# An attention and MoE kernel on one core: the gate is finished inside its PSUM bank

## The chip, the cores and the metric

The kernel runs on one core of one Trainium2 chip. The metric is device time in microseconds (us) of one execution. The kernel before takes 829.81 us, the median of three runs between 829.25 and 830.32 us. One execution was profiled: it took 829.51 us, and its profile spans 827.7 us from the first instruction to the last.

## The reference

The reference computes a linear attention over 8 batches and 8 heads (576 rows of 64 each) and feeds its output, 4608 tokens of 512 numbers, to two matrix products with a gate between them. All inputs and outputs are fp32.

```python
q_s = softmax(q, axis=-1); k_s = softmax(k, axis=2)       # per row; per column over the 576 rows
kv = einsum('bhsd,bhse->bhde', k_s, v)
x = einsum('bhsd,bhde->bhse', q_s, kv)                    # then reordered to 4608 x 512
h = x @ w_in                                              # 512 -> 2048
g = h - np.tanh(h)
out = g @ w_out                                           # 2048 -> 512
```

`softmax` stands here for the max, exp, sum and division that the reference writes out (with 1e-9 added to each sum).

## The kernel before

**Tiles.** The 4608 tokens are nine chunks of 512 (index j). The 2048 hidden columns are 16 blocks of 128 (index f). A step is one pair (j, f). It has two matrix products on TensorE (PE):

- `ph` (line 739): 12 matmuls of 128x512 that write h of the step, transposed, into one PSUM bank. fp32 is carried by two fp32r parts per factor: the parts are `xh`, `xl` of x and `w[0]`, `w[1]` of the weights, and three of the four products are made.
- `po` (line 814): 12 matmuls of 128x512 that add the step's share to four output banks, one per 128 tokens. The gate g comes as two parts, `gh` (rounded to fp32r) and `gl` (the rest).

So a step has 24 matmuls, and 144 steps have 3456.

**The gate of a step** (`h_parts`, lines 719 to 793) is made of ten instructions between the two products. ScalarE (ACT) reads the bank twice (`u` = h squared, `t` = tanh h) and makes `vv` from `u`. VectorE (DVE) makes `tt` (h - tanh h, from the bank), `g` (in place in the bank), `gg` (from the bank to an SBUF tile `g`) and `cp`, a select (COPY_PREDICATED, line 761) that puts `t` into the SBUF tile where the mask `m` of `u` says so. `m` is made on ACT or DVE. Then `gh` casts the SBUF tile (ACT, GpSimd or DVE, line 195) and `gl` subtracts (DVE or GpSimd (POOL), line 775). The bank of `ph` comes free behind `gg`.

**PSUM.** Of the eight banks four are `ps_o` (the outputs `po`; at the program's head also small products, and `ph` of steps 2 and 3), two are `ps_h` (`ph`) and two are `ps_m` (`pm`, `pb`, `pk`, `pt`, `px`: the products of the attention).

**Attention.** For each batch, k is loaded, its column maximum taken (`km`), exponentiated (`ke`), and multiplied with v (`pk`); the sums are divided out (`sl`, `rs`, `rc`, `kn`) into `kvs`. q is loaded, softmaxed by rows (`mq`, `qu`, `qe`, `sq`, `sa`, `sr`, `qn`), turned (`pt` on PE and a copy `qs` to SBUF in the first two chunks, by DMA later) and multiplied with `kvs` (`px`), and `xh`, `xl` are made from `px`. The q, k and v of batches 0 and 1 are worked on at the head of the program; later ones lie between the steps.

**Weights** come as 8-byte words and are turned into two fp32r parts on the chip: `ld` (DMA), `cl` and `pr` (clamp and scale the high words), `lo` (the low words, ACT), `st` (shift and or, DVE), `ca` (cast) and `sub` (the rest). A piece `i0` or `o2` is of `w_in` or `w_out` and begins at that block of 128.

**Order.** The order of all instructions is written out by hand in three texts: FIRST (the head and the first 32 steps), ROUND (16 steps, run for the chunks 2 to 8) and LAST. Each word is one operation; the emission in that order gives every engine its own queue, in order. A mark at a word's end moves it from its home engine: `*` to DVE, `^` to POOL, `!` to ACT. The same order also issues the DMAs, on SyncE's (SP's) queue. PE runs the `po` of a step one to several steps behind its `ph`.

Of the kernel before, what the change touches and what calls it, by code (L numbers as in the profile page):

```python
# [10 lines left out]
F32 = mybir.dt.float32  # L11
F32R = mybir.dt.float32r
# [19 lines left out]
k0.0 km0.a warm1 vo0.2 warm8 warm1 k0.1 km0.b warm3 k0.2 km0.c kk0.1 kk0.3 km0.d q1 vo0.0 kk0.0 pm0  # L32
q0 mq1 vo0.1 mq0 q3 qu1 mx0 kk0.2 warm3 qe1 mq3 ld.i4 qu0 pb0 kl0.1 qe0 vo1.1 ks0.2 sq1 cl.i4^
warm3 sq0 sa1 sa0 kf0.2 v0.2 ke0.1 kl0.3 sr1 sr0 lo.i4 kl0.0 kl0.2 pr.i4 warm3 ke0.0 qu3 qn1* qn0*
ld.i2 warm3 pt1 qe3 ke0.2 pt0 st.i4 v0.0 sq3 pk0.0 ke0.3 v0.1 ca.i4 qs1 ld.i0 cl.i2 sub.i4* qn2*
pk0.2 pk0.1 sa3 lo.i2 qn3 pt3 sl0 sr3 rs0 cl.i0^ qn7 rc0 q2 ld.i1 k1.1 pt2 pr.i2 qs2 qs0* qn6 kn0
qs3 k1.0 st.i2 pr.i0 px0 lo.i0 ca.i2 px2 mq2 warm3 st.i0 sub.i2* vo1.2 xh0.1 xh2.0 pt7 ld.o0 warm3
qu2* xh0.0 xl0.0 km1.a xh2.1 xl0.1 cl.i1^ pt6 k1.2 ca.i0 sub.i0 qe2 ld.o2 v1.1 lo.i1 qs7 xl2.1 pha0
vo1.0 phc2 pha2 qs6 pha3 xl2.0 sq2 km1.b phb0 cl.o0^ pr.i1 phc0 phb2 pr.o0 km1.c st.i1 lo.o0 phb3
km1.d ld.i12 st.o0 u0 ca.i1 t0 pm1 vv0 u2 tt0 sa2 t2 phb1 v1.0 phc3 mx1 g0 tt2 ca.o0 pb1 gg0 m0  # L40
ks1.0 cp0 pha1 sub.i1 cl.o2^ lo.o2 phc1 pr.o2 ke1.0 u1 ks1.1 sr2 ks1.2 phb5 qn4 t1 g2 tt1 ke1.1
phc5 ld.o4 v1.2 vv1 g1 ke1.2 gg1 m1 pha5 pk1.0 qn5* pt4 gh0^ pk1.1 pk1.2 qs4 cp1 sub.o0* vv2 pt5
gl0 po0.1b st.o2 gg2 t3 m2 gh1 phb4 po0.0b po0.0a qs5 sl1 gl1 pha4 po1.0a ld.i6 po1.1a u3 tt3 ca.o2
cl.o4^ rs1 g3 vv3 m3 rc1 gg3 po1.0b po0.3a po1.3a cp2 kn1 sub.o2* po0.1a phc4 lo.o4 po1.2a po1.3b
pr.o4 +q.0 po0.2a po1.2b ld.i8 t4 gh2 po1.1b px4 po0.2b po0.3b u4 cp3 po2.1a st.o4 po2.2a xh4.0
ld.i10 gh3^ xh4.1 po2.3a t5 po3.1a po2.0a tt4 xl4.0 vv4 xl4.1 g4 ld.o6 gl3 gg4 px6 ca.o4 gl2 ld.o8
ld.i15 m4 po3.1b cl.i8 xh6.0 u5 po2.2b po3.3a po3.2b xh6.1 po3.2a sub.o4* cp4 po3.3b cl.i6^ vv5
po3.0b xl6.1 gh4 pr.i8 tt5 po2.3b xl6.0 pha6 po3.0a po4.0a lo.i6 po2.1b phb6 phc6 gl4 g5 gg5 m5*
# [48 lines left out]
phc1 phb0 phc0 pha0 po15.0a u0 +q.0 po15.2a +mq.0 vv0 po15.0b phb1 po14.1a po15.3a +qu.0* t0
po15.3b tt0 g0 pha1 po15.1a t1 po14.0a m0* gg0 cp0 po14.2b u1 po14.3b tt1 po14.0b gh0 phb2 g1 oc.0*
vv1 gg1 +qe.0 pha2 phc2 po0.2a os.0 po14.3a +sq.0 t2 tt2 m1 po15.2b po15.1b po14.1b po14.2a oc.1*
pha3 u2 gl0* vv2 phb3 po0.1b phc3 g2 gg2 m2 phb4 pha4 phc4 cp1 oc.2 po0.2b po0.0a os.1 gh1 oc.3  # L100
po0.1a po0.3a gl1* cp2 +sa.0 po0.3b t3 +k.0 +sr.0 +qn.0* po1.0a po0.0b u3 +k.2 t4 po1.0b gh2 tt3
# [29 lines left out]
def attn_moe_kernel(  # L131
# [9 lines left out]
    nc = tc.nc  # L141
# [919 lines left out]
```

## Time and profile before

| | |
|---|---|
| median of three runs | 829.81 us |
| the profiled execution | 829.51 us, its span 827.7 us |
| PE busy | 816.2 us (99%) |
| DVE busy | 697.9 us (84%) |
| ACT busy | 511.7 us (62%) |
| POOL busy | 87.8 us (11%) |
| chain that ended last | PE 92%, ACT 3%, DMA 2%, the rest 1% each |

Times inside the profile count from the first instruction. A busy PE includes the `warm` products (line 276), which do no work that is needed. Where a view prints a duration, instructions of one engine overlap a little: the next one starts before the one in front has ended, so the distance from start to start is shorter than the duration.

### The profile page before, as it was taken

How to read it: one execution, taken by the hardware profiler on the slowest of the kernel's cores; microseconds unless marked ns; L12 is line 12 of the kernel's file. 1: busy time of each engine (PE TensorE's matmuls, PEld its weight loads, DVE VectorE, ACT ScalarE, POOL GpSimd, SP SyncE). 2: the span in 40 equal slices, each digit the busy share in tenths (PEclk: the TensorE clock that was granted, in tenths of full speed). 3: DMA queues.
4: the chain of work that ended last, by engine and by line, in shares of the span. 5: the costliest groups of instructions: out<-in, count | busy, mean ns of one | idle time of the engine just before them, and what ended most of it. 6: DMA issues, size and time to landing. Idle time of an engine off the chain costs nothing.

```text
span 827.7 us, 13205 instructions
## 1 busy us (share of the span) xinstructions
PE 816.2 (99%) x4830; PEld 705.3 (85%) x4830; DVE 697.9 (84%) x1134; ACT 511.7 (62%) x845; POOL 87.8 (11%) x94
## 2 busy tenths in 40 slices
PE   8899999999999999999999999999999999999997
PEld 7788888888888888888888888888888888888886
DVE  6999999977999789987998789978997897767564
ACT  4899998645555656555656465556555565456553
POOL 4545535301000000000000000000000000000000
PEclk9999999999999999999999999999999999999999
DMA  9974500433221504041314122332304120301001
GB/s 300 357 287 169 172 2 1 128 101 110 71 83 41 145 18 136 13 131 43 98 55 140 47 82 71 102 84 59 95 26 139 34 77 15 123 4 52 1 1 51
DMA packets 99935, 75.83 MB, mean 92 GB/s; under 512 B 17184, under 2 KB 84768, under 8 KB 99872
## 3 DMA queue, kind: packets, MB, share of 16 engines
q1 hardware_dynamic: 99712, 74.74, 29.2%
q8 instruction: 38, 0.62, 0.3%
q10 hardware_dynamic: 160, 0.26, 0.1%
q14 instruction: 25, 0.20, 0.1%
HBM read 56.10 MB, written 18.89 MB: 91 GB/s over the span
## 4 chain that ended last, share of the span: by engine, by line
PE 92%; ACT 3%; DMA 2%; POOL 1%; issue 1%; DVE 1%; SPq 0%; ACTq 0%; POOLq 0%
PE po L814 45%; PE ph L739 43%; PE pk L444 2%; PE px L676 2%; DMA raw_o<-in_moe_w_out_dram 1%; DMA q<-in_q_dram 1%; POOL c_i L225 0%; ACT raw_o L235 0%; ACT c_o L231 0%; PE px L660 0%; ACT k L432 0%; ACT raw_i L235 0%; POOL q L537 0%; ACT c_i L231 0%; ACT u L766 0%
## 5 line engine op out<-in xcount | busy, mean ns | idle before, releaser
L814 PE MATMUL po<-w_o,gh 128*128 128x512 f32 x1152 | 309.8, 379 | 0.3 <-POOL gh L195 0.3
L739 PE MATMUL ph<-xh,w_i 128*128 128x512 f32 x1152 | 283.8, 379 | 0.6 <-ACT w_i L195 0.6
L739 PEld LDWEIGHTS ph<-xh,w_i 128*128 128x128 f32 x1152 | 217.2, 189 | 32.1 <-ACT w_i L195 0.9
L814 PEld LDWEIGHTS po<-w_o,gh 128*128 128x128 f32 x1152 | 217.4, 189 | 31.8 <-POOL gh L195 0.7
L814 PE MATMUL po<-w_o,gl 128*128 128x512 f32 x576 | 185.7, 382 | 0.0
L739 PE MATMUL ph<-xl,w_i 128*128 128x512 f32 x576 | 148.8, 381 | 0.8 <-DVE g L756 0.5
L195 ACT CAST gh<-g 128x512 fp32r<-128x512 f32 x122 | 75.3, 618 | 101.2 <-PE po L814 78.5
L753 DVE TENSOR_TENSOR t<-ph,t 128x512 f32<-128x512 f32 x144 | 97.7, 682 | 45.6 <-ACT t L729 41.3
L729 ACT ACTIVATE t<-ph 128x512 f32<-128x512 f32 x144 | 85.2, 592 | 74.9 <-PE ph L739 70.1
L729 ACT ACTIVATE u<-ph 128x512 f32<-128x512 f32 x144 | 85.1, 591 | 63.3 <-PE ph L739 44.9
L814 PEld LDWEIGHTS po<-w_o,gl 128*128 128x128 f32 x576 | 108.6, 189 | 17.4 <-issue 1.2
L739 PEld LDWEIGHTS ph<-xl,w_i 128*128 128x128 f32 x576 | 107.8, 189 | 18.0 <-PE po L814 1.2
L775 DVE TENSOR_TENSOR gl<-g,gh 128x512 fp32r<-128x512 f32 x128 | 87.2, 684 | 37.1 <-ACT gh L195 18.8
L761 DVE COPY_PREDICATED g<-u,t 128x512 f32<-128x512 int32 x144 | 108.9, 764 | 4.1 <-ACT u L766 2.4
L756 DVE SCALAR_TENSOR_TENSOR g<-vv,ph 128x512 f32<-128x512 f32 x144 | 98.1, 681 | 9.7 <-ACT vv L729 4.3
L729 ACT ACTIVATE vv<-u,b_pa 128x512 f32<-128x512 f32 x144 | 103.8, 721 | 2.6 <-DVE g L756 1.0
L748 DVE SCALAR_TENSOR_TENSOR ph<-u,ph 128x512 f32<-128x512 f32 x144 | 99.3, 689 | 5.8 <-ACT u L729 5.7
L766 ACT ACTIVATE u<-u 128x512 int32<-128x512 f32 x118 | 74.4, 631 | 28.5 <-DVE ph L748 28.1
L304 POOL MEMSET v<- 128x16 f32 x14 | 1.7, 119 | 374.0 <-DVE tb L575 152.1
L195 ACT CAST xh<-px 128x512 fp32r<-128x512 f32 x36 | 20.0, 587 | 13.1 <-PE px L676 13.1
L775 POOL TENSOR_TENSOR gl<-g,gh 128x512 fp32r<-128x512 f32 x16 | 22.1, 1384 | 50.1 <-ACT gh L195 36.3
L717 DVE TENSOR_TENSOR xl<-px,xh 128x512 fp32r<-128x512 f32 x36 | 23.9, 685 | 3.2 <-ACT xh L195 3.2
(117 smaller groups left out, 553.0 us busy)
## 6 DMA issues: line engine op xcount, KB each, us to landing
k<-in_k_dram SPq DMA_DIRECT2D x16, 512.0 KB, 4.3
q<-in_q_dram SPq DMA_DIRECT2D x15, 512.0 KB, 5.3
v<-in_v_dram SPq DMA_DIRECT2D x14, 512.0 KB, 5.6
qd<-tb SPq DMA_DIRECT2D x28, 256.0 KB, 3.2
out_dram<-o SPq DMA_DIRECT2D x28, 256.0 KB, 2.3
qs<-qd SPq DMA_DIRECT2D x112, 64.0 KB, 2.0
raw_i<-in_moe_w_in_dram SPq DMA_DIRECT2D x6, 1024.0 KB, 8.2
raw_o<-in_moe_w_out_dram SPq DMA_DIRECT2D x6, 1024.0 KB, 10.6
```

The lines of the kernel that those rows point to most:

```text
L195: (eng.copy if eng is nc.scalar else eng.tensor_copy)(to, of)
L444: nc.tensor.matmul(st["pk"][hh * D : (hh + 1) * D, a, j : j + D + 1], kt[:, h, j] if u < NKP else kt[:, h], vt[:, h, j * (D + 1) : (j + 1) ...
L717: nc.vector.tensor_tensor(xl, px, xh.bitcast(F32), op=ALU.subtract)
L729: nc.scalar.activation(new(tag, **of), st[src], fn, **kw)
L739: nc.tensor.matmul(pairs(st["ph"]), w[:, i, c], halves(xs[j][x][:, c, :]), start=n == 0, stop=n == 3 * NC - 1,)
L748: nc.vector.scalar_tensor_tensor(st["ph"], st["u"], C2, st["ph"], op0=ALU.mult, op1=ALU.mult)
L753: nc.vector.tensor_tensor(st["t"], st["ph"], st["t"], op=ALU.subtract)
L756: nc.vector.scalar_tensor_tensor(new("g"), st["vv"], PB, st["ph"], op0=ALU.add, op1=ALU.mult)
L761: nc.vector.copy_predicated(st["g"], st["mk"], st["t"])
L766: eng.activation(mk, st["u"], AF.Copy, scale=0.5 / U_MAX)
L775: eng.tensor_tensor(new("gl", F32R), st["g"], st["gh"].bitcast(F32), op=ALU.subtract)
L814: nc.tensor.matmul(pairs(po[key]), gs[j, f][g][:, cols], halves(wt["o", f][:, w]), start=n == 1, stop=n == last,)
```

## The change

The SBUF tile `g` goes. `gg` and `cp` now write the bank of `ph` itself, and `gh` and `gl` read it there, so a bank comes free only behind `gl`. POOL does not take part any more: `gl` is always on DVE, and `gh` on ACT or DVE. `ps_h` and `ps_m` become one ring of four banks, from which the small products take theirs too; `ph` of steps 2 and 3 no longer uses `ps_o`. The room of the SBUF tiles `g` goes to a third buffer of `dec` (the weights' work tiles and the output tiles). The last two output tiles are copied whole by one engine each and not in two halves. FIRST and ROUND are new texts; of LAST one mark is gone.

```diff
 FIRST = """
-k0.0 km0.a warm1 vo0.2 warm8 warm1 k0.1 km0.b warm3 k0.2 km0.c kk0.1 kk0.3 km0.d q1 vo0.0 kk0.0 pm0
+q0 mq0 qu0* warm8 k0.0 vo0.2 qe0 warm3 k0.1 warm3 warm3 kk0.1 km0.a km0.b k0.2 q1 warm3 km0.c mq1
...
 LAST = """
-po142.2a po142.2b po143.2a po143.2b oc8.2* os8.2 po142.3a po142.3b po143.3a po143.3b oc8.3 os8.3
+po142.2a po142.2b po143.2a po143.2b oc8.2 os8.2 po142.3a po142.3b po143.3a po143.3b oc8.3 os8.3
...
-    ps_h = ctx.enter_context(tc.tile_pool(name="ps_h", bufs=2, space=bass.MemoryType.PSUM))
-    ps_m = ctx.enter_context(tc.tile_pool(name="ps_m", bufs=2, space=bass.MemoryType.PSUM))
+    ps_h = ctx.enter_context(tc.tile_pool(name="ps_h", bufs=4, space=bass.MemoryType.PSUM))
-    dec = ctx.enter_context(tc.tile_pool(name="dec", bufs=2))
+    dec = ctx.enter_context(tc.tile_pool(name="dec", bufs=3))
...
         def gg():
             nc.vector.scalar_tensor_tensor(
-                new("g"), st["vv"], PB, st["ph"], op0=ALU.add, op1=ALU.mult
+                st["ph"], st["vv"], PB, st["ph"], op0=ALU.add, op1=ALU.mult
             )
         def cp():
-            nc.vector.copy_predicated(st["g"], st["mk"], st["t"])
+            nc.vector.copy_predicated(st["ph"], st["mk"], st["t"])
...
         def gh(eng):
-            cast_on(eng, new("gh", F32R), st["g"])
+            cast_on(eng, new("gh", F32R), st["ph"])
-        def gl(eng):
-            eng.tensor_tensor(
-                new("gl", F32R), st["g"], st["gh"].bitcast(F32), op=ALU.subtract
+        def gl():
+            nc.vector.tensor_tensor(
+                new("gl", F32R), st["ph"], st["gh"].bitcast(F32), op=ALU.subtract
             )
...
         elif j == NCH - 1 and t >= TPC - 2:
             o = gp.tile([P, DM], F32, name=f"o{j}_{t}", tag="t")
-            to, of = by_half(o), paired(po[key])
-            nc.scalar.copy(to[:, 0], of[:, 0])
-            nc.vector.tensor_copy(to[:, 1], of[:, 1])
+            cast_on(eng, by_half(o), paired(po[key]))
```

**The loads of the head, on SP's queue.** `k1_0` and `k1_1` are the two large tiles of k of batch 1, `raw_i` and `raw_o` pieces of the weights. Before:

```order
L203 DMA raw_i0_281<-in_moe_w_in_dram 128x4x128
L517 DMA q1_0_332<-in_q_dram 128x8x128
L203 DMA raw_i1_334<-in_moe_w_in_dram 128x4x128
L282 DMA k1_1_336<-in_k_dram 128x8x128
L282 DMA k1_0_350<-in_k_dram 128x8x128
L208 DMA raw_o0_396<-in_moe_w_out_dram 128x2x512
L287 DMA kr1_416<-in_k_dram 64x8x64
L208 DMA raw_o2_422<-in_moe_w_out_dram 128x2x512
```

Now:

```order
L517 DMA q1_0_275<-in_q_dram 128x8x128
L314 DMA v0_0_216<-in_v_dram 128x8x128
L203 DMA raw_i4_318<-in_moe_w_in_dram 128x4x256
L208 DMA raw_o0_342<-in_moe_w_out_dram 128x2x512
L282 DMA k1_1_391<-in_k_dram 128x8x128
L282 DMA k1_0_414<-in_k_dram 128x8x128
L287 DMA kr1_416<-in_k_dram 64x8x64
L314 DMA spare_v1_273<-in_v_dram 128x8x128
```

The loads of batch 1's k have moved behind a piece of `w_out` and a piece of `w_in`; the rows ahead of these hold the same other tiles in both.

**The head of DVE's queue, from the row maximum of batch 1 (`mx1`) on.** `ph0_0` is h of step (0, 0), `c_i` and `c_o` are work tiles of the weights. Before:

```order
L377 TENSOR_REDUCE mx1_511<-pm1_487 128x4
L748 SCALAR_TENSOR_TENSOR ph0_0_429<-u0_0_481,ph0_0_429 128x512
L753 TENSOR_TENSOR t0_2_499<-ph0_2_436,t0_2_499 128x512
L756 SCALAR_TENSOR_TENSOR g0_0_522<-vv0_0_492,ph0_0_429 128x512
L429 TENSOR_TENSOR k1_0_350<-k1_0_350,pb1_517 128x1024
L761 COPY_PREDICATED g0_0_522<-u0_0_481,t0_0_485 128x512
L429 TENSOR_TENSOR k1_1_336<-k1_1_336,pb1_517 128x1024
L558 RECIPROCAL sq1_0_497<-sq1_0_497 128x16
L429 TENSOR_TENSOR kr1_416<-kr1_416,pb1_517 64x512
L748 SCALAR_TENSOR_TENSOR ph0_2_436<-u0_2_494,ph0_2_436 128x512
L753 TENSOR_TENSOR t0_1_553<-ph0_1_501,t0_1_553 128x512
L748 SCALAR_TENSOR_TENSOR ph0_1_501<-u0_1_541,ph0_1_501 128x512
```

Now:

```order
L377 TENSOR_REDUCE mx1_502<-pm1_483 128x4
L747 SCALAR_TENSOR_TENSOR ph0_0_433<-u0_0_469,ph0_0_433 128x512
L755 SCALAR_TENSOR_TENSOR ph0_0_433<-vv0_0_479,ph0_0_433 128x512
L752 TENSOR_TENSOR t0_1_471<-ph0_1_438,t0_1_471 128x512
L760 COPY_PREDICATED ph0_0_433<-u0_0_469,t0_0_463 128x512
L747 SCALAR_TENSOR_TENSOR ph0_1_438<-u0_1_498,ph0_1_438 128x512
L755 SCALAR_TENSOR_TENSOR ph0_1_438<-vv0_1_513,ph0_1_438 128x512
L553 TENSOR_REDUCE sq1_0_536<-sums_eps_97 128x16
L774 TENSOR_TENSOR gl0_0_538<-ph0_0_433,gh0_0_517 128x512
L760 COPY_PREDICATED ph0_1_438<-u0_1_498,t0_1_471 128x512
L752 TENSOR_TENSOR t0_2_531<-ph0_2_474,t0_2_531 128x512
L774 TENSOR_TENSOR gl0_1_557<-ph0_1_438,gh0_1_544 128x512
```

The gates' instructions on one bank stand closer together, each `gl` is now in this queue, and the subtractions of batch 1's k have moved behind them.

**POOL's queue in the same stretch.** `w_o0` is the fp32r tile of the first piece of `w_out`, `qn4` and `qn5` are scaled q tiles of the second chunk. Before:

```order
L225 TENSOR_SCALAR c_o0_458<-raw_o0_396 128x1024
L255 TENSOR_TENSOR w_i1_483<-c_i1_409,w_i1_483 128x512
L225 TENSOR_SCALAR c_o2_532<-raw_o2_422 128x1024
L604 TENSOR_TENSOR qn4_551<-q1_0_332,sq1_0_497 128x2x4x64
L195 CAST gh0_0_600<-g0_0_522 128x512
L775 TENSOR_TENSOR gl0_0_637<-g0_0_522,gh0_0_600 128x512
L775 TENSOR_TENSOR gl0_1_661<-g0_1_569,gh0_1_647 128x512
L225 TENSOR_SCALAR c_o4_678<-raw_o4_562 128x1024
L195 CAST gh0_3_747<-g0_3_687 128x512
L775 TENSOR_TENSOR gl0_3_766<-g0_3_687,gh0_3_747 128x512
```

Now:

```order
L225 TENSOR_SCALAR c_o0_421<-raw_o0_342 128x1024
L195 CAST w_o0_488<-c_o0_421 128x1024
L255 TENSOR_TENSOR w_o0_488<-c_o0_421,w_o0_488 128x1024
L255 TENSOR_TENSOR w_i4_500<-c_i4_399,w_i4_500 128x1024
L225 TENSOR_SCALAR c_o2_549<-raw_o2_446 128x1024
L225 TENSOR_SCALAR c_i8_600<-raw_i8_453 128x1024
L195 CAST w_o2_608<-c_o2_549 128x1024
L255 TENSOR_TENSOR w_o2_608<-c_o2_549,w_o2_608 128x1024
L604 TENSOR_TENSOR qn5_615<-q1_0_275,sq1_0_536 128x2x4x64
L604 TENSOR_TENSOR qn4_699<-q1_0_275,sq1_0_536 128x2x4x64
```

POOL no longer makes `gh` or `gl`; casts and subtractions of the weights, which DVE and ACT made, have come in their place.

## Rows read from the trace of the kernel before

**Rows 1.** The page, part 1: busy time (share of the span) and instructions.

```profile
PE 816.2 (99%) x4830; PEld 705.3 (85%) x4830; DVE 697.9 (84%) x1134; ACT 511.7 (62%) x845; POOL 87.8 (11%) x94
```

**Rows 2.** Stretches of 20 us: busy time and instructions (x) of each engine; clock; DMA.

```profile
40.00:60.00 20.00, 19.82 (x176) 16.29 (x175) 19.56 (x33) 19.92 (x31) 9.32 (x9) 1.00 0.79 281
...
480.00:500.00 20.00, 20.00 (x95) 17.50 (x94) 18.42 (x32) 13.18 (x22) 0.00 (x0) 1.00 0.28 86
```

**Rows 3.** Waits of PE: engine, line, waited for: us in total, times, longest.

```profile
...
PE ph L739 <- DVE g L756: 0.5, 1, 0.5
PE pm L338 <- ACT raw_o L235: 0.4, 1, 0.4
PE po L814 <- POOL gh L195: 0.3, 1, 0.3
...
```

**Rows 4.** PE in order of time: start, us, line, out<-in, count.

```profile
30.48 3.77 PE L739 MATMUL ph<-xh,w_i 128*128 128x512 f32 x16 [0.62 <-ACT w_i L195]
...
57.90 1.09 PE L660 MATMUL px<-spare_qs,kvs 64*64 64x256 f32 x16
```

**Rows 5.** The chain that ended last, 20 to 36 us: start, us, what.

```profile
24.52 9.27 DMA raw_o<-in_moe_w_out_dram
...
33.94 1.58 POOL c_o L225
```

**Rows 6.** DVE in order of time, 40 to 46 us: start, us, line, operation.

```profile
40.79 0.69 DVE L748 SCALAR_TENSOR_TENSOR ph<-u,ph 128x512 f32<-128x512 f32 x1
41.39 0.69 DVE L753 TENSOR_TENSOR t<-ph,t 128x512 f32<-128x512 f32 x1
...
42.58 1.22 DVE L429 TENSOR_TENSOR k<-k,pb 128x1024 f32<-128x1024 f32 x1
43.71 0.76 DVE L761 COPY_PREDICATED g<-u,t 128x512 f32<-128x512 int32 x1
44.36 1.21 DVE L429 TENSOR_TENSOR k<-k,pb 128x1024 f32<-128x1024 f32 x1
```

**Rows 7.** Groups by line and form: busy, mean ns | idle before, and releasers.

```profile
L761 DVE COPY_PREDICATED g<-u,t 128x512 f32<-128x512 int32 x144 | 108.9, 764 | 4.1 <-ACT u L766 2.4
...
L717 DVE TENSOR_TENSOR xl<-px,xh 128x512 fp32r<-128x512 f32 x36 | 23.9, 685 | 3.2 <-ACT xh L195 3.2
...
L775 DVE TENSOR_TENSOR gl<-g,gh 128x512 fp32r<-128x512 f32 x128 | 87.2, 684 | 37.1 <-ACT gh L195 18.8 <-PE po L814 10.3 <-ACT u L766 7.0
...
L195 ACT CAST gh<-g 128x512 fp32r<-128x512 f32 x122 | 75.3, 618 | 101.2 <-PE po L814 78.5 <-DVE g L761 19.8 <-DVE sl L457 1.1
...
L195 ACT CAST xh<-px 128x512 fp32r<-128x512 f32 x36 | 20.0, 587 | 13.1 <-PE px L676 13.1
...
L195 DVE COPY o<-po 128x512 f32<-128x512 f32 x15 | 10.3, 687 | 2.6 <-PE po L814 2.6
...
L195 ACT COPY o<-po 128x512 f32<-128x512 f32 x15 | 8.6, 574 | 1.5 <-PE po L814 1.5
...
L195 DVE CAST gh<-g 128x512 fp32r<-128x512 f32 x14 | 5.8, 414 | 0.0
...
L255 POOL TENSOR_TENSOR w_i<-c_i,w_i 128x1024 fp32r<-128x1024 f32 x2 | 4.8, 2414 | 0.0
```

**Rows 8.** All engines in order of time, near 158 us.

```profile
158.03 1.28 POOL L429 TENSOR_TENSOR kr<-kr,mrow 64x512 f32<-64x512 f32 x1
...
158.28 1.65 DVE L761 COPY_PREDICATED g<-u,t 128x512 f32<-128x512 int32 x1
...
159.81 0.68 DVE L753 TENSOR_TENSOR t<-ph,t 128x512 f32<-128x512 f32 x1
```

**Rows 9.** All engines in order of time, the last microseconds.

```profile
822.92 0.37 ACT L839 COPY o<-po 128x256 f32<-128x256 f32 x1 [1.08 <-PE po L814]
823.33 0.42 DVE L840 COPY o<-po 128x256 f32<-128x256 f32 x1 [1.03 <-ACT o L839]
823.78 0.50 ACTq L850 DMA_DIRECT2D out_dram<-o  x1
```

More of the change, by code (lines that the diff above doesn't have):

```diff
@@ L37 @@
[L37 to L48, printed above, removed]
@@ new lines @@
+t1 km1.d pha2 vv0 st.o0 tt0 pm1 ca.o0^ phb2 phc2 u1 ca.i4 mx1 g0 phb3 sub.o0 m0 gg0 vv1 tt1 cp0 gh0
+phc3 pha3 g1 sub.i4 gg1 v1.2 t2 po0.0a sa2 gl0 m1 cp1 u2 gh1 po0.3a cl.o2^ vv2 u3 tt2 v1.0 gl1
+po0.1a g2 pr.o2 po0.2a pb1 po0.3b po1.0a ks1.2 po1.1b po1.3b phb4 po0.2b lo.o2 ks1.0 m2 ks1.1 phc4
+t3 st.o2 ke1.2 pha4 cl.i8^ sr2 gg2 cp2 po1.2a ke1.1 ca.o2^ sub.o2 ke1.0 vv3 po0.0b qn5 tt3 gh2
+po1.0b po1.3a g3 po1.2b t4 pk1.2 pk1.1 pk1.0 gl2 sl1 m3 gg3 lo.i8 u4 rs1 rc1 po1.1a po2.3b po2.0a
+pt5 cp3 ld.o4 kn1 ld.i10 po0.1b qs5 qn4 ld.i6 gh3* vv4 pha5 tt4 gl3 +vo.2 cl.o4^ g4 pt4 pr.i8 qs4*
@@ L94 @@
+gl30
 """
 ROUND = """
[L97 to L101, printed above, removed]
@@ L334, in kv_max_t @@
     def kv_max_t(b: int, st: dict):
-        st["pm"] = pm = ps_m.tile([P, NC, P], F32, name=f"pm{b}", tag="m")
+        st["pm"] = pm = ps_h.tile([P, NC, P], F32, name=f"pm{b}", tag="h")
         km = st["km"].rearrange("p h d -> p (h d)")
@@ L380, in kv_rows @@
     def kv_rows(b: int, st: dict):
-        pb = ps_m.tile([P, NC, P], F32, name=f"pb{b}", tag="m")
+        pb = ps_h.tile([P, NC, P], F32, name=f"pb{b}", tag="h")
         for a in range(NC):
@@ L438, in kv_mm @@
         if n == 0:
-            st["pk"] = ps_m.tile([P, NC, D + 2], F32, name=f"pk{b}", tag="m")
+            st["pk"] = ps_h.tile([P, NC, D + 2], F32, name=f"pk{b}", tag="h")
         kt, vt = st.pop(("k", u)), st.pop(("v", u))
@@ L595, in q_psum @@
             return ps_o.tile([P, NC, P], F32, name=name, tag="o")
-        return ps_m.tile([P, NC, P], F32, name=name, tag="m")
+        return ps_h.tile([P, NC, P], F32, name=name, tag="h")
     def q_norm(i: int, eng):
@@ L732, in ph @@
             if "ph" not in st:
-                pool, tag = (ps_o, "o") if j == 0 and f in (2, 3) else (ps_h, "h")
-                st["ph"] = pool.tile([P, CH], F32, name=f"ph{j}_{f}", tag=tag)
+                st["ph"] = ps_h.tile([P, CH], F32, name=f"ph{j}_{f}", tag="h")
             w = wt["i", f]
@@ L1019, in run @@
                         key = f"{part}{n}{key[len(bare):]}"
-                if key == f"gl{len(steps) - 1}":
-                    name = key + "*"
                 go(key + name[len(name.rstrip("*!^")) :], ops[key])
```

151 lines of the change are left out of this document (81 added, 70 removed).

## The prediction

> **What bounds the kernel now.** The page's busy times come first: PE is busy for 816.2 of 827.7 us and DVE for 697.9, so PE is the bound, with DVE next [rows 1]. The table by stretches then shows two regimes. Between 480 and 500 us PE is busy throughout and starts 95 instructions, one in 0.21 us, so a full stretch of matmuls runs at one in some 0.216 us; POOL does nothing there and DVE is busy for 18.42 of 20 us. Between 40 and 60 us DVE (19.56) and ACT (19.92) are full as well, with POOL at 9.32 [rows 2]. The reader is to see that the rounds have nothing left on PE but small waits, and that the head is where three engines fight. The view of PE's waits says how small the waits are: behind the first step there are 0.5 us for a bank (released by `gg`, line 756), 0.4 us for `pm` and 0.3 us for a `gh` on POOL [rows 3]. The timeline of PE gives two marks: the first `ph` starts at 30.48 us, and the first `px` of the second chunk at 57.90 us [rows 4]. The chain of waits says what the loads do: `raw_o0` lands at 24.52 + 9.27 = 33.79 us, and POOL starts on it at 33.94 [rows 5].
>
> The matmuls of the steps are the same 3456 in both kernels. So the change can move the end in three places only: how far PE has come at the end of the head, what it waits for later, and the tail.
>
> **The head.** By SP's rows, `k1_0` is now the load that stands where `raw_o0` stood, with the same tiles ahead of it in another order. The queue was full there, so I let it land when `raw_o0` landed, at 33.8 us [rows 5]. DVE's `km` of batch 1 begins with it, and behind that all gates stand in DVE's queue in order. From `km` to the copy `spare_qs` of the second chunk, which the first `px` of that chunk needs, there are 41 instructions on DVE. By the starts of a full stretch, one of 512 elements takes 0.60 us (40.79 to 41.39), one of 1024 takes 1.13 (42.58 to 43.71), a select 0.65 (43.71 to 44.36) [rows 6]. So 26 x 0.60 + 4 x 0.65 + 5 x 1.13 = 23.9; the five small ones and `kn` are 0.9 by my estimate, between none and six of 0.60. Sum 24.8, and the `px` could start at 33.8 + 24.8 = 58.6 us. PE has by then made 97 matmuls of steps, where it had 94 before at 57.90 [rows 4], by counting its rows; `pt`, `pk`, `pm` and `pb` are the same. So PE is behind by 58.6 - 57.9 - 3 x 0.216 = 0.05 us: nothing, if DVE never waits.
>
> It will wait. Selects have two inputs in SBUF, and a select that meets a POOL instruction is long: at 158.28 us one took 1.65 us where the mean is 0.764 [rows 7], beside a POOL instruction that ended at 158.03 + 1.28 = 159.31; the next DVE instruction started at 159.81, 0.5 us after that [rows 8]. So the select began its work when POOL was done. In the new POOL queue, a subtraction of 1024 elements (2.41 us [rows 7]) stands at each of `w_o0` and `w_i4`, another at `w_o2`, then `qn5`, `qn4`. Laid beside DVE's queue by the same durations, POOL is inside `w_o0`'s subtraction when the first select is due (0.5 us lost), inside the cast of `w_o2` at the third (0.3), and inside `qn5` at the fourth (0.7); the second falls on the border. That is 1.5 us, so the `px` starts near 60.1 and PE is behind by 1.55 us. From there on DVE and PE run neck and neck for some twenty microseconds, with POOL still full of weights: I add 0.5 us, less than one such meeting, because DVE then gains on PE. It costs nothing if the selects fall between POOL's instructions, and up to 0.9 us each (1.65 less 0.764) if all do not.
>
> The Trainium skill speaks against the change at this place: "SBUF — State Buffer", section "SBUF: two separate sides", says that VectorE instructions with two SBUF inputs and GpSimd instructions that read SBUF take a shared port pair as an exclusive lock, for the whole instruction. The trace agrees by the select of 1.65 us at 158.28 us [rows 8]. By that rule a meeting with a subtraction of 2.41 us would cost up to its whole length; three such meetings at half the length would make 3.6 us out of my 1.5, and the time 832.9.
>
> **The gate's own instructions.** `gg` writes PSUM; the neighbour in that form is `g` of line 748, with starts 0.60 us apart like the others [rows 6]: nothing. `gl` reads the bank: `xl`, which reads PSUM too, takes 685 ns where `gl` took 684 [rows 7]: nothing. `gh` on ACT from PSUM: `xh` takes 587 ns where `gh` took 618 [rows 7]; ACT is off the path in the rounds, so nothing. `gh` on DVE from PSUM: a copy from `po` takes 687 where the cast from SBUF took 414 [rows 7], and there are now 35 of them for 14, so DVE has 24.0 us for 5.8. `gl` adds 16 on DVE, 10.9 us. Against that, of the forms with 0.7 us or more each, DVE gives seven q subtractions, five k, seven weight subtractions and eight output copies to other engines, some 27 us by their own durations. DVE ends at about the 697.9 us it had; it has 1.5 us free in every 20 of the rounds [rows 2], and none is needed. The select's form with its output in PSUM is not in the trace. The nearest rows give 0.68 us (a DVE instruction on PSUM) below and 0.764 above without POOL, 1.65 with [rows 7, 8]; I take 0.764, as the bank is free of other engines then.
>
> **The banks.** A bank is held longer, but there are four. In ROUND, the rows of PE between the last matmul of a `ph` and the first of the next tile in its bank are 48 matmuls at least, 48 x 0.216 = 10.4 us; before they were 22, 4.8 us, and had to cover the gate as far as `gg`. Behind `gg` come `cp`, `gh`, `gl` alone, 0.76 + 0.62 + 0.68 = 2.1 us [rows 7]. So the cover grows by 5.6 us and the need by 2.1: the bank's wait of 0.5 us [rows 3] should go, and the wait for a `gh` on POOL (0.3) cannot come back, as POOL makes none. I take 0.8 us off. Two small products (`px`) take two of the four banks twice in a round; this is in the 48.
>
> **The tail.** The last tile is copied by ACT from 822.92 and then by DVE to 823.33 + 0.42 = 823.75, one behind the other [rows 9]. One whole copy on ACT takes 0.574 [rows 7], to 823.49: 0.26 us less. The store's issue follows at once in both. The tile before it is off the path.
>
> **Sum**, on the profiled execution: 829.51 + 1.55 + 0.5 - 0.8 - 0.26 = 830.5 us. It stands 0.3 us under the median of 829.81, so the forecast is 830.8 us: no change that can be told, which here means within 0.2% (1.66 us), 828.15 to 831.47.
>
> **The rivals.**
>
> *The selects meet POOL nearly every time* (slower). The place is DVE's queue between 38 and 100 us, the price up to 0.9 us for each select, and it decides from the point where DVE's loss is more than 2.5 us, since that would put the sum above 831.47. For it speaks that POOL's queue now holds a subtraction or cast of weights behind nearly every step of the head, against it that DVE's own waits let POOL pass, as in the kernel before, where the mean of all 144 selects is 0.764 us beside the 1.65 of the long one [rows 7, 8]. Four selects before the `px` at 0.9 us are 3.6 in place of 1.5, and half as much behind it, 1.8 in place of 0.5: 829.81 + 0.05 + 3.6 + 1.8 - 1.06 = 834.2 at its worst, 832.8 at two thirds. Chance 0.30.
>
> *The head loses nothing* (faster). DVE finds its gaps, the `px` starts at 58.6, and the three small waits of PE go: 829.81 + 0.05 - 0.8 - 0.4 - 0.26 = 828.4; with the first `ph` 0.4 us earlier, as its weights `raw_i0` are now loaded ahead of v, 828.0. For it speaks that PE's waits of the head are of the old order, against it that POOL's work in the head has grown. Chance 0.18.
>
> *The ring does not give what it says* (slower). If a bank is short once in a round, it is seven times: 0.3 us a round, the size of a wait in [rows 3], make 2.1 us and 832.9. Against it speak the 48 matmuls. Chance 0.07.
>
> **How the numbers follow.** The forecast has 0.45, the rivals 0.30, 0.18 and 0.07. The forecast's own range is 829.3 to 832.0. The range from 828.2 to 833.6 reaches into both sides and leaves out the worst of the selects and the best of the head, about a tenth at each end. Faster by over 0.2%: 0.18. Within: 0.45. Slower: 0.37, which is the two slower rivals.
>
> **What would show it.** In the profile after, the first `px` of the second chunk starts near 60 us, with PE idle before it and DVE without a gap from about 34 us; selects of over 1 us stand beside POOL's subtractions there, some three before 60 us. `km` of batch 1 starts at 33.8 us, when `k1_0` lands. In the rounds PE shows no wait for a bank, each round is as long as before, and a select takes 0.76 us. The last copy takes 0.57 us. It is wrong if a round is longer by 0.2 us or more, if a select in the rounds is far from 0.76 us, or if `km` starts away from 34 us.

## The result, and the profile after

The changed kernel takes 839.02 us (838.78 to 840.20), the kernel before 829.53 on the same chips: 1.0119 times as long (95% interval 1.0102 to 1.0137), 9.5 us slower. The forecast was 830.8 us, the range 828.2 to 833.6. The time lies well outside it.

The page's busy times of the changed kernel answer to [rows 1]. PE has hardly more work; DVE has 11 us more in 26 more instructions, and POOL 21 us more.

```profile
PE 817.2 (98%) x4830; PEld 703.9 (84%) x4830; DVE 709.0 (85%) x1160; ACT 486.6 (58%) x812; POOL 108.5 (13%) x99
```

The table by stretches answers to [rows 2]. In the rounds PE is full as before. DVE's 15.80 us here stand against 18.42, but the slice falls on another part of a round than before: from 230 to 800 us DVE is busy for 474.3 of 570 us, and was for 476.5. PE has lost its time earlier.

```profile
40.00:60.00 20.00, 18.75 (x158) 15.26 (x157) 19.59 (x33) 18.21 (x28) 16.29 (x11) 1.00 0.59 195
...
480.00:500.00 20.00, 20.00 (x109) 17.41 (x100) 15.80 (x26) 13.11 (x24) 0.00 (x0) 1.00 0.12 42
```

One row of 80 us tells more than forty slices. The same view from 80 to 160 us, of the kernel before:

```profile
80.00:160.00 80.00, 79.68 (x369) 69.27 (x369) 77.72 (x118) 68.48 (x105) 39.49 (x29) 1.00 0.22 66
```

and of the changed kernel:

```profile
80.00:160.00 80.00, 74.29 (x339) 63.04 (x338) 78.33 (x117) 57.78 (x92) 35.01 (x25) 1.00 0.33 98
```

DVE looks as full in both, with one instruction less; ACT and POOL have less to do; and PE has started 30 instructions fewer. DVE is busy for as long and gets less done.

PE's waits answer to [rows 3] (engine, line, what it waited for: us in total, times, longest). The three small waits of before are gone, and larger ones for the gate have come.

```profile
PE po L813 <- ACT gh L195: 2.6, 2, 2.0
PE po L813 <- DVE gh L195: 2.3, 2, 1.2
PE pm L338 <- DVE km L332: 1.9, 1, 1.9
...
PE ph L738 <- DVE gl L774: 1.5, 1, 1.5
PE px L660 <- DVE kvs L465: 1.2, 1, 1.2
...
PE po L813 <- DVE gl L774: 1.2, 3, 0.7
```

PE's two marks answer to [rows 4]: the first `ph` starts 1.83 us later, the first `px` of the second chunk 3.25 us later.

```profile
32.31 1.99 PE L738 MATMUL ph<-xh,w_i 128*128 128x512 f32 x8
...
61.15 1.09 PE L660 MATMUL px<-spare_qs,kvs 64*64 64x256 f32 x16
```

Where the time went is seen best by counting. The 24 x n-th matmul of the steps starts, in the changed kernel against the one before (worked out from all `ph` and `po` rows of PE in both traces):

```
step n            0      5     10     12     16     22   rounds 2-3  last
us later      +1.83  +2.60  +2.21  +6.12  +8.05 +10.47     +10.47   +9.54
```

So 2.2 us are lost up to 95 us, 8.3 us between 95 and 165 us, and 1 us is won back in the rounds; 0.7 of it at the one place where the kernel before waited for a bank (448.36 us) and this one does not. Between 95 and 165 us PE waits six times for `gh` or `gl` (1.98, 1.50, 0.28, 1.07, 0.67 and 1.20 us, 6.7 in all). Behind 170 us PE waits for nothing for which the view of waits has a row.

The timeline of all engines at 94 us shows what happens in the stretch that was lost:

```profile
94.54 2.42 POOL L255 TENSOR_TENSOR w_o<-c_o,w_o 128x1024 fp32r<-128x1024 f32 x1
94.65 2.87 DVE L760 COPY_PREDICATED ph<-u,t 128x512 f32<-128x512 int32 x1
...
97.61 0.59 ACT L195 CAST gh<-ph 128x512 fp32r<-128x512 f32 x1 [2.02 <-DVE ph L760]
...
98.24 0.70 PE L813 MATMUL po<-w_o,gh 128*128 128x512 f32 x2 [1.98 <-ACT gh L195]
```

POOL's subtraction starts 0.11 us ahead of DVE's select and ends at 96.96. The select, counted as busy for 2.87 us, ends 0.56 us after that, so its work was done when POOL had finished. ACT idles for 2.02 us ahead of `gh`, and PE for 1.98 ahead of `po`. The same distance stands at 42.47, 120.61 and 160.97 us: these selects end 0.55 to 0.57 us behind a POOL instruction of 2.4 us. In all, 15 instructions of DVE are longer than the median of their own group (same line and shapes) by over 0.15 us, and each stands beside POOL. They are called meetings below, and what they are over is their cost: 11.6 us together (11 meetings and 5.9 us in the kernel before). Ten of them are selects, with 8.7 us.

The groups answer to [rows 7] (line, engine, operation, shapes, count | busy, mean ns | idle before). The prices of the gate's own edits came out as forecast, but POOL's subtraction of 1024 elements is there nine times for two.

```profile
L760 DVE COPY_PREDICATED ph<-u,t 128x512 f32<-128x512 int32 x144 | 108.5, 758 | 4.3 <-ACT u L765 0.7
...
L774 DVE TENSOR_TENSOR gl<-ph,gh 128x512 fp32r<-128x512 f32 x144 | 98.6, 686 | 45.2 <-PE po L813 37.1 <-ACT gh L195 4.9 <-ACT u L729 0.4
...
L195 ACT CAST gh<-ph 128x512 fp32r<-128x512 f32 x109 | 64.0, 587 | 76.0 <-DVE ph L760 40.2 <-PE po L813 35.3 <-DVE ph L755 0.4
...
L195 DVE CAST gh<-ph 128x512 fp32r<-128x512 f32 x35 | 24.0, 686 | 3.2 <-PE po L813 2.6
...
L255 POOL TENSOR_TENSOR w_o<-c_o,w_o 128x1024 fp32r<-128x1024 f32 x5 | 12.4, 2478 | 4.4 <-ACT w_o L195 4.0
...
L255 POOL TENSOR_TENSOR w_i<-c_i,w_i 128x1024 fp32r<-128x1024 f32 x4 | 10.1, 2519 | 10.9 <-DVE w_i L195 10.9
```

The tail answers to [rows 9]: the store is issued 0.61 us behind the copy's start, and 1.03 us behind the start of the last matmul.

```profile
831.89 0.38 PE L813 MATMUL po<-w_o,gl 128*128 128x512 f32 x1
832.31 0.59 ACT L195 COPY o<-po 128x512 f32<-128x512 f32 x1 [0.71 <-PE po L813]
832.92 0.50 ACTq L847 DMA_DIRECT2D out_dram<-o  x1
```

### The profile page after: what moved, and what is told of

The parts are those of the page before. It is cut to its first block, busy times and chain, and to the rows that moved or that the text cites. A ratio compares the mean times of both kernels' runs of the same rounds, so it can differ in the third digit from the quotient of the medians.

```text
span 837.1 us, 13152 instructions
## 1 busy us (share of the span) xinstructions
PE 817.2 (98%) x4830; PEld 703.9 (84%) x4830; DVE 709.0 (85%) x1160; ACT 486.6 (58%) x812; POOL 108.5 (13%) x99
## 4 chain that ended last, share of the span: by engine, by line
PE 82%; DVE 8%; issue 2%; ACT 2%; POOL 1%; DVEq 0%; ACTq 0%; POOLq 0%
PE po L813 40%; PE ph L738 38%; PE pk L444 2%; PE px L676 2%; DVE ph L760 2%; DVE gl L774 1%; DVE ph L747 1%; DVE t L752 1%; DVE ph L755 1%; DVE c_o L238 0%; DVE c_i L238 0%; DVE gh L195 0%; ACT t L729 0%; POOL w_o L255 0%; PE px L660 0%
## 5 line engine op out<-in xcount | busy, mean ns | idle before, releaser
L738 PE MATMUL ph<-xh,w_i 128*128 128x512 f32 x1152 | 288.9, 380 | 1.6 <-DVE gl L774 1.5
L813 PE MATMUL po<-w_o,gl 128*128 128x512 f32 x576 | 188.1, 382 | 1.2 <-DVE gl L774 1.2
L774 DVE TENSOR_TENSOR gl<-ph,gh 128x512 fp32r<-128x512 f32 x144 | 98.6, 686 | 45.2 <-PE po L813 37.1
L760 DVE COPY_PREDICATED ph<-u,t 128x512 f32<-128x512 int32 x144 | 108.5, 758 | 4.3 <-ACT u L765 0.7
L195 ACT CAST gh<-ph 128x512 fp32r<-128x512 f32 x109 | 64.0, 587 | 76.0 <-DVE ph L760 40.2
L755 DVE SCALAR_TENSOR_TENSOR ph<-vv,ph 128x512 f32<-128x512 f32 x144 | 99.2, 689 | 9.1 <-ACT vv L729 4.1
L765 ACT ACTIVATE u<-u 128x512 int32<-128x512 f32 x104 | 63.9, 628 | 30.0 <-DVE ph L747 29.8
L537 POOL TENSOR_TENSOR q<-q,mq 128x1024 f32<-128x1024 f32 x9 | 17.7, 1970 | 231.7 <-DVE mq L532 231.6
L195 DVE CAST gh<-ph 128x512 fp32r<-128x512 f32 x35 | 24.0, 686 | 3.2 <-PE po L813 2.6
L432 ACT ACTIVATE k<-k 128x1024 f32<-128x1024 f32 x14 | 14.6, 1050 | 15.3 <-DVE k L429 9.4
```

The costliest lines, as they stand in the source:

```text
L195: (eng.copy if eng is nc.scalar else eng.tensor_copy)(to, of)
L537: eng.tensor_tensor(qf, qf, mq, op=ALU.subtract)
L738: nc.tensor.matmul(pairs(st["ph"]), w[:, i, c], halves(xs[j][x][:, c, :]), start=n == 0, stop=n == 3 * NC - 1,)
L755: nc.vector.scalar_tensor_tensor(st["ph"], st["vv"], PB, st["ph"], op0=ALU.add, op1=ALU.mult)
L760: nc.vector.copy_predicated(st["ph"], st["mk"], st["t"])
L765: eng.activation(mk, st["u"], AF.Copy, scale=0.5 / U_MAX)
```

## The experiments

Theory A: DVE instructions that meet POOL wait until it is done, and POOL's new work meets them. Theory B: DVE simply has more to do, as `gl` and more `gh` are its own. The kernel before, timed beside each run, took 827.8 to 828.2 us there; so ratios to it are compared. The changed kernel's is 1.0119.

### POOL's weights left out, its casts given to ACT

```diff
 def clamp(eng):
+    if eng is nc.gpsimd: return          # scale then reads words(1)
 def cast(eng):
+    eng = nc.scalar if eng is nc.gpsimd else eng
 def rest(eng):
+    if eng is nc.gpsimd: return          # the matmuls read w[:, 0] again
```

> The changed kernel, with the weights' work that POOL does left out: no clamp where POOL made it (scale reads the raw words), no low part where POOL made it (the matmuls read the high part again), and POOL's casts made by ACT. DVE's queue is the same, instruction for instruction. Theory A (meetings: a DVE instruction with two SBUF inputs that meets a POOL instruction waits until that ends; the trace of the changed kernel has 15 such DVE instructions, 11.6 us over the usual length, ten of them selects): all but those beside q and k work on POOL go, so 6 to 8 us of 839.0 go, 831 to 833 us, and step 32 stands 2.5 to 4.5 us behind the kernel before in place of 10.5. Theory B (load: DVE has more to do in the head, as gl and more gh are its own now, and PE waits for a full DVE): the same DVE work, so 838 to 840.

Measured: 836.89 us, 1.0109 (1.0092 to 1.0126). Only 2.6 us of long DVE instructions were left, but the time hardly fell: a miss for theory A as it was put (831 to 833), and below the range of theory B (838 to 840) too. The timeline shows why. ACT was busy for 66.1 us between 80 and 160 us (57.8 in the changed kernel), and a cast of weights that had been POOL's now stood ahead of `gh`:

```profile
97.41 1.08 ACT L195 CAST w_o<-c_o 128x1024 fp32r<-128x1024 f32 x1
...
98.97 0.62 ACT L195 CAST gh<-ph 128x512 fp32r<-128x512 f32 x1
...
99.64 0.70 PE L821 MATMUL po<-w_o,gh 128*128 128x512 f32 x2 [1.01 <-ACT gh L195]
```

The run took away one wait and put another in its place; it decides nothing until it is made without that (below).

### One input of the select in SBUF

```diff
-nc.vector.copy_predicated(st["ph"], st["mk"], st["t"])
+nc.vector.tensor_tensor(st["ph"], st["ph"], st["t"], op=ALU.max)
```

> The changed kernel, with each of the 144 selects replaced by a two-input maximum of the PSUM bank and t (the mask is left out), which has one input in SBUF and one in PSUM; the other instructions on PSUM of this kind take 0.68 us, beside POOL or not. Theory A: the selects' 8.7 us of excess go, and some 6 to 8 us of the time, 831 to 833 us; the long shift (2.6 us at 105 us) and the long products of q stay. Theory B: the instruction takes 0.68 us for 0.70, so nothing: 838 to 840.

Measured: 829.21 us, 1.0015 (1.0005 to 1.0024). More came back than expected (831 to 833): 10.4 of the 11.9 thousandths. POOL works as before (104.8 us), DVE has the same queue, and none of the 144 is long:

```profile
L760 DVE TENSOR_TENSOR ph<-ph,t 128x512 f32<-128x512 f32 x144 | 98.8, 691 | 1.5
```

The step table ends at +0.10 us. Theory B falls: the same number of instructions of the same length are DVE's load here.

### POOL's weights in pieces of 256

```diff
-eng.tensor_tensor(w[:, 1], c, w[:, 0], op=ALU.subtract)     # and the clamp, the cast
+for a, b in cuts(eng):                                      # 256 columns each on POOL
+    eng.tensor_tensor(w[:, 1, a:b], c[:, a:b], w[:, 0, a:b], op=ALU.subtract)
```

> The changed kernel, with every clamp, cast and subtraction of weights on POOL cut into pieces of 256 columns (four for 1024), the same work in the same order. Theory A, if a waiting DVE instruction gets in between two POOL instructions: a meeting costs at most one piece, some 0.7 us in place of up to 2.2, no select over 1.6 us beside weights' work, and 3 to 5 us go: 834 to 836 us. If DVE must wait until POOL's queue has a gap: the longest selects stay at 2.5 us or grow, and the time is 839 or more, since POOL's pieces take some 25% longer in all. Theory B: 838 to 840.

Measured: 841.39 us, 1.0159 (1.0143 to 1.0174). Half of the expectation holds: no select beside weights' work is over by more than 0.53 us, so a waiting DVE instruction does get in between two of POOL's. The time expected for that case (834 to 836) was missed: there were 20 meetings with 10.2 us, the longest beside the uncut work on q and k, and POOL was busy for 130.2 us. Its slower clamps made ACT late, and with it DVE:

```profile
77.55 2.50 POOL L231 TENSOR_SCALAR c_i<-raw_i 128x256 f32<-128x256 f32 x3
...
80.08 1.06 ACT L238 ACTIVATE c_i<-c_i 128x1024 f32<-128x1024 f32 x1 [2.98 <-POOL c_i L231]
...
83.25 0.70 DVE L765 SCALAR_TENSOR_TENSOR ph<-vv,ph 128x512 f32<-128x512 f32 x1 [2.33 <-ACT vv L739]
```

### gh off DVE

```diff
-... gh3* ... gh4* ... gh31*      (14 words of FIRST)
+... gh3 ... gh4 ... gh31
```

> The changed kernel, with the 14 gh of the first 32 steps that DVE makes put on ACT, 0.60 us of DVE's time each (five of them between 66 and 165 us, where PE waits for DVE). Theory B: DVE's load there falls by 3.0 us, and the time by 3 us or more, to 836 or less. Theory A: the selects move against POOL's instructions, which are the same, so meetings change by chance; with 3 us less load but the same meetings 837 to 839.

Measured: 841.20 us, 1.0157 (1.0142 to 1.0173). Less load on DVE made it slower, not 3 us faster, which speaks against theory B; but the time is above the 837 to 839 of theory A too. The five largest meetings stand almost as they stood (2.14, 0.92, 1.37, 1.78, 1.47 us over). The run is not clean, as ACT got what DVE gave: PE now waits longer for `gh` on ACT (2.6 us in the changed kernel).

```profile
PE po L813 <- ACT gh L195: 4.9, 4, 2.0
```

### POOL's weights left out, ACT as it was

```diff
 def clamp(eng):
+    if eng is nc.gpsimd: return          # scale reads raw[:, :M], times 0
 def rest(eng):
+    if eng is nc.gpsimd: return          # POOL keeps its casts
```

> As the run without POOL's weights, but with ACT's queue left as it is in the changed kernel: POOL keeps its casts, scale reads contiguous words (and multiplies by 0, so these weights are only low words), POOL's clamps and subtractions are left out. In the earlier run ACT had got POOL's casts and slow strided reads, and PE's waits there were for gh on ACT. Theory A (a two-SBUF-input instruction of DVE waits for POOL's instruction): meetings with 1 us casts and with q and k work remain, 3 to 5 us on DVE in place of 11.6; 831 to 834 us. If the 2.1 us of the earlier run were all that POOL's weights cost: 836 to 838.

Measured: 829.01 us, 1.0015 (1.0006 to 1.0025), less than the 831 to 834 expected: the first run of this kind made clean. Three long instructions with 1.9 us are left, and PE is full between 80 and 160 us:

```profile
80.00:160.00 80.00, 79.93 (x370) 69.61 (x369) 76.59 (x129) 60.74 (x96) 11.38 (x10) 1.00 0.33 98
```

Taking away POOL's half of the meeting gives the same time as taking away DVE's half.

### Two inputs in SBUF, but no select

```diff
-nc.vector.copy_predicated(st["ph"], st["mk"], st["t"])
+nc.vector.tensor_tensor(st["ph"], st["mk"].bitcast(F32), st["t"], op=ALU.max)
```

> The changed kernel, with each select replaced by a two-input maximum of the mask and t, both in SBUF, written to the PSUM bank (the gate's value is lost). Same length by itself as the maximum that reads the bank and t (829.2 us), and it waits for the mask as the select does. Theory A: two inputs in SBUF are what meets POOL, so the meetings are back, instructions of 1.5 us and more beside POOL, 837 to 841 us. Rival D (the select as an operation, or its wait, is slow beside POOL, not the two inputs): no meetings, 829 to 831 us.

Measured: 838.73 us, 1.0132 (1.0117 to 1.0147). The meetings are back at the same places, so the operation does not matter, and where its inputs lie does:

```profile
94.61 2.38 POOL L255 TENSOR_TENSOR w_o<-c_o,w_o 128x1024 fp32r<-128x1024 f32 x1
94.74 2.81 DVE L760 TENSOR_TENSOR ph<-u,t 128x512 f32<-128x512 f32 x1
```

One rival is left by the two maxima: the fast one does not wait for the mask, and this one does. The run above settles it: it keeps the select, the mask and the wait (4.3 us idle before the selects, as in the changed kernel), and takes 829.01 us.

### v first in the head

```diff
-vo1.1 q2 qu3 kf0.2 v0.0 qe3 ... cl.i1^ mq2 ld.i4 ... px0 qu2
+vo1.1 v0.0 q2 qu3 kf0.2 qe3 ... cl.i1^ ld.i4 ... px0 mq2 qu2
```

> The changed kernel, with v0.0 loaded ahead of the first q tile of batch 1 and that tile's row maximum put behind the first px on DVE. In the changed kernel v0.0 lands at 24.8 us (19.7 before) and the row maximum stands ahead of sl, so that kvs is ready at 28.5 and the first ph starts at 32.31 (30.48 before). Theory A with this as the head's own term: first ph near 31 us, and 1 to 1.5 us of the time, 837.5 to 838. Rival (DVE has no gap from 34 us on, so an earlier first ph is given back): 838.5 to 839.5.

Measured: 843.28 us, 1.0179 (1.0160 to 1.0198). A miss on both sides: the first `ph` started at 34.47 us. POOL's subtraction of q2, moved with its maximum, ran from 28.55 to 30.87 us, and DVE's `qn` at 29.03 took 2.38 us beside it.

### POOL started behind a select

```diff
+def pw(): nc.gpsimd.memset(st["u"][:, :1], 0.0)      # must wait until cp has read it
-sub.o6 ... sub.o13 ... +qn.1 ... sub.o8 ... +ks.0^
+pw9 sub.o6 ... pw11 sub.o13 ... pw12 +qn.1 ... pw13 sub.o8 ... pw20 +ks.0^
```

> The changed kernel, with a tiny memset on POOL ahead of five of its instructions (the subtractions of w_out pieces 6, 13 and 8, the scaling of q for the third chunk, the subtraction of k for batch 2), which overwrites a word of the mask that the select before has read: POOL starts these when a select has just ended, and the next select is some 5 us away. Those five met selects for 7.1 us in all. Theory A: the five meetings go, some of it comes back in others, 832 to 835 us, with the same work on every engine. Rival (POOL only falls behind, and the meetings move to other instructions or the weights come late): 838 to 840.

Measured: 836.77 us, 1.0109 (1.0094 to 1.0124): 2.3 us less than the changed kernel by trace (+7.27 at the last step for +9.54). None of the five selects is long any more, but other instructions take their places:

```profile
94.62 0.70 DVE L760 COPY_PREDICATED ph<-u,t 128x512 f32<-128x512 int32 x1
...
95.44 0.10 POOL L779 MEMSET u<- 128x1 f32 x1 [1.01 <-DVE ph L760]
95.49 2.41 POOL L255 TENSOR_TENSOR w_o<-c_o,w_o 128x1024 fp32r<-128x1024 f32 x1
...
97.86 1.54 POOL L225 TENSOR_SCALAR c_o<-raw_o 128x1024 f32<-128x1024 f32 x1
97.91 2.04 DVE L238 SCALAR_TENSOR_TENSOR c_o<-c_o,raw_o 128x512 uint32<-128x512 uint32 x1
...
159.54 2.38 POOL L429 TENSOR_TENSOR k<-k,mrow 128x1024 f32<-128x1024 f32 x1
160.07 2.13 DVE L767 TENSOR_SCALAR u<-u 128x512 int32<-128x512 f32 x1
```

The time lies between the two ranges (832 to 835; 838 to 840), and the rival was partly right: five such new meetings have 5.6 us, in place of the 7.1 that went.

### The kernel before with the new division of work

```diff
-sub.o0* ca.o2 gh3^ ca.i6^ ...      (FIRST of before)
+sub.o0 ca.o2^ gh3* ca.i6* ...      (63 words as in the changed kernel; every gl on DVE)
```

> The kernel before, in its own order and with its own banks, but in the first 32 steps the weights' clamps, casts and subtractions and the gate's gh go to the engines that the changed kernel gives them, and every gl to DVE (63 words of FIRST with another engine). POOL then works on weights where it worked on gates. Theory A (what POOL works on decides: gh and gl begin when a select has ended, weights begin at any time and meet it): instructions of DVE that meet POOL lose 9 us or more in place of 5.9, PE waits between 60 and 165 us appear, and the time is 832 to 840 us. Rival (the new order or the ring is what costs, not the division): 827 to 830.

Measured: 861.71 us, 1.0401 (1.0385 to 1.0417), beyond both. POOL is busy for 87.3 us, as before (87.8), but the long DVE instructions are 25 and have 23.4 us over, four times as much. Eleven of them are `gl`, which in this kernel still reads two SBUF tiles:

```profile
66.79 2.39 POOL L255 TENSOR_TENSOR w_o<-c_o,w_o 128x1024 fp32r<-128x1024 f32 x1
66.85 2.89 DVE L775 TENSOR_TENSOR gl<-g,gh 128x512 fp32r<-128x512 f32 x1
...
69.79 0.62 PE L814 MATMUL po<-w_o,gl 128*128 128x512 f32 x1 [2.28 <-DVE gl L775]
```

The queue of before was written for another division, and DVE has more to do than before (721.6 us for 697.9), so not all 33 us are meetings. Shown is that the new division alone, without the new order and the ring, brings them, with POOL busy for as long.

### The control: POOL out of the kernel before

The edit is the one of the clean run, in the kernel before.

> The control for the run with POOL's clamps and subtractions left out: the same edit in the kernel before. Theory A: DVE's 5.9 us of meetings there stand where PE hardly waits (its waits behind the first ph are some 2 us in all), so 826 to 828.5 us, at most 2 us of gain. Rival (leaving the work out is worth some 10 us by itself, since weights are ready earlier): well under 826.

Measured: 826.85 us, 0.9981 (0.9972 to 0.9991), as theory A says. Leaving the work out, with the meetings it had there, is worth about 1.5 us by the ratio (2.4 by the spans of the two traces) where PE hardly waited for the meetings, so it does not explain the 10 thousandths it gave in the changed kernel.

### The head again, alone and with the gates

```diff
 (alone, with the move of v0.0 of the run above)
-... cl.i1^ mq2 ld.i4 ... px0 qu2 sr3 qn6 st.i1 qn7* qe2 ca.i1 px2 warm3 sq2 k1.1 ... xl2.0 cl.i4^ xh0.0 pt7 ... km1.c pr.o0
+... cl.i1^ ld.i4 ... px0 sr3 qn6 st.i1 qn7* mq2 ca.i1 px2 warm3 k1.1 ... xl2.0 qu2 cl.i4^ xh0.0 qe2 pt7 ... km1.c sq2 pr.o0
```

> The changed kernel, with v0.0 loaded ahead of q2 and the row maximum, subtraction and exponential of q2 put behind the first px and behind the qn on DVE that met POOL in the earlier run of this kind (29.0 us, 2.4 us long). Theory A for the head: kvs earlier by a microsecond, first ph at 31.0 to 31.5 us in place of 32.31, and 0.8 to 1.3 us of the time if the meetings behind it stay as they are: 837.7 to 838.3. Rival: another qn or the km meets the moved subtraction on POOL, and the first ph is no earlier: 839 to 841.

> Both repairs in the changed kernel: the head's order of the run beside this one and the five POOL instructions that wait for a select. If both effects stand by themselves: 836.8 less 0.8 to 1.3, 835.5 to 836. If the head's change moves the meetings: 836.5 to 839.

Measured: 841.95 us, 1.0164 (1.0149 to 1.0180) alone, and 839.82 us, 1.0139 (1.0124 to 1.0154) with the gates. Both times lie above both ranges expected. Alone, the first `ph` did start at 31.35 us, as expected. Then POOL's queue, pushed back by the moved subtraction, met DVE's `km` and the shift behind it, three times in a row:

```profile
34.25 1.72 POOL L255 TENSOR_TENSOR w_i<-c_i,w_i 128x512 fp32r<-128x512 f32 x1
34.85 1.66 DVE L329 TENSOR_TENSOR km<-km,k 128x512 f32<-128x512 f32 x1
35.93 2.02 POOL L225 TENSOR_SCALAR c_o<-raw_o 128x1024 f32<-128x1024 f32 x1
...
36.70 2.33 DVE L238 SCALAR_TENSOR_TENSOR c_i<-c_i,raw_i 128x1024 uint32<-128x1024 uint32 x1 [0.18 <-ACT c_i L231]
```

The gates gave 2.1 us here as well. No version made here beats the kernel before with the whole computation done. Pairing the order of before with the ring was not tried.

## Why the prediction was wrong

**The step that failed** is in the part on the head: "From there on DVE and PE run neck and neck for some twenty microseconds, with POOL still full of weights: I add 0.5 us", with the bound "up to 0.9 us each (1.65 less 0.764)". The mechanism was named rightly, and was the largest rival besides; it was mis-sized twice. The term of 0.5 us stands for all meetings behind the `px`; between 95 and 165 us alone they cost 8.3 us.

- **The price.** 0.9 us was read from a select that met an instruction of 1.28 us [rows 8]. What a meeting costs is what is left of POOL's instruction, and the subtraction of 2.41 us stood in [rows 7]. The forecast even said that the select "began its work when POOL was done", and did not carry it to the length of the new work. Measured: up to 2.17 us for a select. With this price the rival's worst, 834.2 us, would have come out far higher.
- **The place.** The rival looked from 38 to 100 us. POOL works on weights to 160 us and on k to 163, DVE is full there (78.33 of 80 us), and 8.3 of the 10.5 us were lost from 95 us on. In the two runs that come out at 1.0015, steps 10 to 22 lose 0.2 and 0.4 us in place of these 8.3.

**What hid the meetings in the kernel before** was put down to DVE's own waits, that "let POOL pass". The runs point elsewhere: the same POOL load with the new division costs 23.4 us of meetings in before's own order. In the trace of before, none of the eleven long DVE instructions ends behind a `gh` or `gl` of POOL, though POOL has 24 of these; all eleven end behind its work on weights, q or k. POOL's gate work there comes out of the gate, `gl` behind `gh` and `gh` behind a select, so it starts when that select is over; weights start whenever their loads and casts are done. That this is the reason is argued from the order of the instructions and not shown; shown is that the new division of work brings the meetings (1.0401), and that starting five POOL instructions behind a select frees these five selects.

**The rule weighed in the prediction** was priced at 832.9 us, with three meetings at half of 2.41 us. It is the Trainium skill's, "SBUF — State Buffer", section "SBUF: two separate sides", and the traces agree with it: the block lasts for the rest of POOL's instruction (ends 0.55 to 0.57 us behind POOL's, four times), strikes the two-input maximum with both inputs in SBUF (2.81 us at 94.74 us) and not the one with an input in PSUM (691 ns mean over 144), and leaves `gl`, now reading PSUM, alone (686 ns mean over 144). What was wrong was the number of meetings given to it.

**Point by point, the rest.** `km` of batch 1 was to start at 33.8 us: 34.15, with `k1_0` landing at 33.81. The `px` near 60.1: 61.15. Some three long selects before it: 1.04, 0.87 and 1.16 us. No loss ahead of the first `ph`: wrong, 1.83 us. Rows of the changed kernel's head point to two causes, `v` landing late and DVE's row maximum `mq` ahead of `sl`:

```profile
24.88 1.15 PE L444 MATMUL pk<-v,k 128*64 128x65 f32 x32 [0.46 <-DMA v<-in_v_dram]
25.06 1.20 DVE L532 TENSOR_REDUCE mq<-q 128x16 f32<-128x1024 f32 x1
...
27.53 0.15 DVE L457 TENSOR_SCALAR sl<-pk 128x4 f32<-128x4 f32 x1
...
28.69 1.09 PE L660 MATMUL px<-spare_qs,kvs 64*64 64x256 f32 x16 [1.24 <-DVE kvs L465]
```

The run that undid both (with three more words moved) gave 0.96 us of it back (31.35); what the rest is stays open. DVE's busy time was to stay at about 697.9 us: 709.0, of which 5.7 are longer meetings. The banks: 0.8 us forecast, 0.97 measured in the rounds, with no wait for a bank. The gate's edits: `gl` 686 ns for 685 forecast, `gh` 587 on ACT and 686 on DVE for 587 and 687; the select by itself 0.70 us for 0.764. The tail: 0.26 forecast, 0.40 from the last matmul's start to the store's issue, of which 0.15 is left in the spans. One sum is off in the forecast itself: the rival of the selects comes by its own terms to 832.4 us at two thirds, not 832.8.

**The sum by its terms**, in us of the traces: head +2.2 at step 10 (2.05 forecast), meetings from 95 to 165 us +8.3 (nothing forecast behind the first twenty), banks -0.97 (-0.8), tail about -0.15 (-0.26): 9.4, against spans of 837.1 and 827.7. That the head came out near its forecast is in part luck. In the two runs that come out at 1.0015 the first `ph` is as late (2.16 and 1.84 us), and yet only 0.87 and 0.79 us are left of it at step 10. So of the 2.2 us some 1.4 are meetings, by this estimate, and the rest is the late start, which the forecast had put at nothing.

## What to carry to other kernels

Before giving work to GpSimd, list what VectorE does in the same stretch with all of its inputs in SBUF, two-input instructions above all, and price each meeting at the rest of the GpSimd instruction, not at what an earlier, shorter one cost. An engine's share of busy time hides this, since a blocked instruction counts as busy: compare the length of single instructions with the median of their group, and look at what PE started in the stretch. Moving such work by hand moves the meetings; what took them away was an input in PSUM, or GpSimd's work out of the stretch.

## What was not expected of the hardware

- A one-input instruction of DVE was blocked as well: the mask (TENSOR_SCALAR 128x512 in SBUF, 0.42 us alone) took 2.13 us at 160.07 us in the run with the gates, ending 0.28 us behind POOL's subtraction.
- POOL pays too: its clamp of 1024 took 2.01 and 2.11 us at 104.85 and 106.83 us of the changed kernel, where its group's mean is 1.6 us, beside DVE instructions that ran in between.
- POOL's casts block: `gl` with two SBUF tiles took 1.52 us at 106.89 us in the kernel before with the new division, beside a cast from 106.40 to 107.86.
